# One 64 KB-per-partition load of wq, one loop for q, and matmuls on zeros ahead of q and of the scores

## The chip, the core and the metric

The kernel runs on one core of a Trainium2 chip. The metric is the device time of one execution in microseconds (us). Before the change three runs gave 98.8, 98.8 and 98.97 us; the median is 98.8 us. One further execution was recorded by the hardware profiler, and all rows below come from it.

## What is computed

One token (x has 1024 elements, all data bf16) goes through an attention branch and an MLP branch, and both are added to it:

```python
xn = layernorm(x)
q = xn @ wq                       # 1024 x 4096: 32 heads of 128
k, v = the last W = 4096 positions of the caches, 4 KV heads, each used by 8 query heads
p = softmax(q k^T * 128 ** -0.5)
attn = (p v) @ wo                 # 4096 x 1024
y = layernorm(xn)
mlp = gelu(y @ w1 + b1) @ w2 + b2 # 1024 x 3584 x 1024
out = x + attn + mlp
```

All of wq (8 MB), K and V (4 MB each), w1 and w2 (7 MB each) and wo (8 MB) must be read from the device memory: 39.86 MB in the profile. The arithmetic on one token is small beside that.

## The kernel before, in words

**Loads.** Nearly every load is issued by SP, in program order, into one queue. Each is one transfer over 128 partitions with one run of bytes per partition; `load_chunks` cuts a weight into chunks of rows. The order on SP is: the first half of wq (32 KB per partition), the first half of K (`load_k(0)`), the second half of wq, the second half of K, w1 (56 KB per partition), then V in two halves, w2 in two chunks, wo in four chunks (`WO_CHUNKS`), and the output. V is loaded into the buffer of K (`KV`), so SP waits for the last of the four transposes of K, `C["kt", 3]`, before V. w2 overwrites wq (both are in `BIG`), so SP waits for eight counts of `done["q"]`; wo overwrites w1, so SP waits for seven counts of `done["h"]`. Three small rows (x, b2 and b1) are issued by ACT on a queue of its own. Both queues are served by the same 16 DMA engines; each takes 8 of the 128 partitions of a large load.

**Engines.** POOL fills constants. ACT zeroes the PSUM banks 0, 1 and 7 by copying a zero tile. PE spreads x over 128 partitions with two matmuls (L426), DVE computes the layernorm statistics and puts the normalized x into `XZ` (L274): a zero tile of 136 columns for each of eight groups, in which a few columns hold x. PE multiplies windows of `XZ` with wq to get q in bank 7: 64 matmuls with a moving operand of 512 columns, in two passes over the halves of wq. A register named `turn` and a semaphore `s_feed`, which POOL raises as loads and transposes finish, let PE wait for the right stage inside a loop; the first two turns are the halves of wq.

DVE transposes K in four pieces (`turn_k`, L284), 4.4 us each, as the halves land: pieces 0 and 1 need the first half of K, 2 and 3 the second. Program order on DVE is piece 0, 1, 2, then the transpose of q (L292) and the copies into `QBD` (L303; ACT makes the other half, L305), then piece 3. The scores on PE are 32 matmuls in two groups of 16: the first needs `QBD` and pieces 0 and 1, the second piece 3. Ahead of them PE does four small matmuls for b1 (L446), two for x and b2 (L454) and four that write the mask of the two KV heads (L457, moving operand with 2 rows).

After the scores PE does w1 (56 matmuls, the loop that counts `done["h"]`), the sum of p, the turned h, p v (32 matmuls), seven rounds of eight matmuls on w2 and four rounds on the first chunk of wo, paced by `s_feed`, and at last the other chunks of wo: matmuls of 32 columns of weights (`OT`), one `s_wo` wait for each chunk; the last chunk, a single row of wo, uses weights that were loaded in advance (L517, L507). Then ACT and DVE copy the result out and SP stores it.

Of the kernel before, what the change touches and what calls it, by code (L numbers as in the profile page):

```python
# [18 lines left out]
KC = D // 128  # L19
NQ = HQ * DH  # L20
W1_CHUNKS = [8]
WQ_CHUNKS = [4, 4]
W2_CHUNKS = [16, 12]
WO_CHUNKS = [16, 11, 4, 1]
WO_HEAD = 1
XW = 136
PAIRS = 2
# [24 lines left out]
def bass_parallel_sum__sliding_block_cached__mixer_channel_mlp__decode_kernel(  # L52
# [17 lines left out]
    pe, dve, act, pool, sp = nc.tensor, nc.vector, nc.scalar, nc.gpsimd, nc.sync  # L70

    def sems(name, n):
        return [nc.alloc_semaphore(f"{name}{i}") for i in range(n)]

    s_x, s_b1, s_b2, s_v, s_out = (nc.alloc_semaphore(n) for n in ("s_x", "s_b1", "s_b2", "s_v", "s_out"))
    s_w1 = sems("s_w1", len(W1_CHUNKS))
    s_wq = sems("s_wq", len(WQ_CHUNKS))
    s_k = sems("s_k", PAIRS)
    s_wo = sems("s_wo", len(WO_CHUNKS))
    s_w2 = sems("s_w2", len(W2_CHUNKS))  # L80

    DVE = Track(nc, "S_DVE")
    ACT = Track(nc, "S_ACT")
    POOL = Track(nc, "S_POOL")
    done = {n: nc.alloc_semaphore(f"S_PE_{n}") for n in (
        "x", "h", "hT", "q", "sc", "pv", "tot", "fin")}
    s_feed = nc.alloc_semaphore("S_FEED")

    def sb(name, shape, d):
        return nc.alloc_sbuf_tensor(name, shape, d)  # L90
# [10 lines left out]
    OTHER = sb("OTHER", [2, 128], bf16)  # L101
    ALT = sb("ALT", [2, 512], bf16)
# [9 lines left out]
    XZ = sb("XZ", [128, KC * XW], bf16)  # L112
    YZ = sb("YZ", [128, 192], bf16)
    QBD = sb("QBD", [128, PAIRS * 512], bf16)
# [16 lines left out]
    GO = sb("GO", [128, ROUNDS * STEP + LEAD + 96], bf16)  # L131
# [6 lines left out]
    WA, W1 = BIG[:, 0:KC * NQ], BIG[:, KC * NQ:KC * NQ + KC * F]  # L138
    W2 = WA[:, 0:FC * D]
    PS = nc.alloc_psum_tensor("PS", [128, 8 * 512], f32)  # L140
    PSb = PS[:, :].bitcast(bf16)

    def bank(n, rows=128, first=0):
        return PS[first:first + rows, n * 512:(n + 1) * 512]

    w1_p = B_w1.rearrange("(p r) n -> p r n", r=KC)
    wq_p = A_wq.rearrange("(p r) n -> p r n", r=KC)
# [5 lines left out]
    C = {}  # L153

    def load_chunks(dst, src, chunks, width, semaphores, c0=0):
        for j, n in enumerate(chunks):
            sp.dma_start(  # L157
                dst[:, c0 * width:(c0 + n) * width].rearrange("p (c n) -> p c n", c=n),
                src[:, c0:c0 + n, :],
            ).then_inc(semaphores[j], 16)  # L160
            c0 += n
# [10 lines left out]
    def pool_wait():  # L172
        pool.wait_ge(POOL.sem, POOL.cnt)
# [53 lines left out]
    def pairs(cache, c):  # L227
        return cache[0, 2 * c:2 * c + 2, SK - W:SK, :].rearrange("g (m i) d -> m g (i d)", m=64)

    def load_k(c):  # L230
        sp.dma_start(KV[:, c * 8192:(c + 1) * 8192], pairs(A_k_cache, c)).then_inc(s_k[c], 16)  # L231

    load_chunks(WA, wq_p, WQ_CHUNKS[:1], NQ, s_wq)
    load_k(0)
    load_chunks(WA, wq_p, WQ_CHUNKS[1:], NQ, s_wq[1:], WQ_CHUNKS[0])
    load_k(1)
    load_chunks(W1, w1_p, W1_CHUNKS, F, s_w1)

# [59 lines left out]
    for b in range(4):  # L298
        for c in range(PAIRS):
            to = QD[32 * b:32 * b + 32, c, :, b, 16 * c:16 * c + 16].rearrange("p e (u j) -> p e u j", j=4)  # L300
# [5 lines left out]
    turn_k(3)  # L306

    V = KV[:, :]
    sp.wait_ge(DVE.sem, C["kt", 3])
    for c in range(PAIRS):  # L310
        sp.dma_start(V[:, c * 8192:(c + 1) * 8192], pairs(A_v_cache, c)).then_inc(s_v, 16)
    sp.wait_ge(done["q"], 8)
    load_chunks(W2, w2_p, W2_CHUNKS, D, s_w2)
    sp.wait_ge(done["h"], 7)
    c0 = 0
    for j, n in enumerate(WO_CHUNKS):
        first = (FC + c0) * D
# [79 lines left out]
    for engine, track, a in ((act, ACT, 1), (dve, DVE, 0)):  # L397
        engine.wait_ge(done["fin"], 1)
        of, to = PS[64 * a:64 * a + 64, 7 * 512 + 256 * a:7 * 512 + 256 * a + 256], Pb[0:64, 256 * a:256 * a + 256]
# [4 lines left out]


    pool_wait()
    pool.wait_ge(s_wq[0], 16)
    pool.sem_inc(s_feed, 1)
    pool.wait_ge(s_wq[1], 16)
    pool.sem_inc(s_feed, 1)  # L410
    pool.wait_ge(DVE.sem, C["kt", 1])
    pool.sem_inc(s_feed, 1)
    pool.wait_ge(DVE.sem, C["kt", 3])
    pool.sem_inc(s_feed, 1)
    for semaphores, chunks in ((s_w2, W2_CHUNKS), (s_wo, WO_CHUNKS[:WO_HEAD])):
        if semaphores is s_wo:
            pool.wait_ge(ACT.sem, C["OT"])
        for semaphore, n in zip(semaphores, chunks):
            pool.wait_ge(semaphore, 16)
            pool.sem_inc(s_feed, n // ROUND)  # L420
    pe.wait_ge(POOL.sem, C["ones"])
    turn = pe.alloc_register("turn")
    pe.reg_mov(turn, 1)
    pe.wait_ge(s_x, 16)
    for i in range(2):
        last = pe.matmul(bank(2 + i), lhsT=onesb[0:1, :], rhs=XB[0:1, 8 * i:8 * i + 8, :])  # L426
    last.then_inc(done["x"], 1)

    def add(to, lhsT, rhs, **place):
        return pe.matmul(to, lhsT=lhsT, rhs=rhs, start=False, stop=False, skip_group_check=True, **place)  # L430

    pe.wait_ge(DVE.sem, C["xz"])
    with pe.Fori(0, len(WQ_CHUNKS)) as j:
        pe.wait_ge(s_feed, turn)
        pe.reg_add(turn, turn, 1)
        with pe.Fori(0, 4) as t:
            for u in range(2):
                for k in range(4):
                    last = add(bank(7), XZ[:, bass.ds(t * 2 + j * (4 * XW) + (XW * k + u), 128)],
                               WA[:, bass.ds(t * -1024 + j * (4 * NQ) + (k * NQ + (7 - u) * 512), 512)])  # L440
            last.then_inc(done["q"], 1)

    pe.wait_ge(s_b1, 16)
    turned = PS[:, 2 * 512 + 32:2 * 512 + 64].rearrange("p (c t) -> p c t", c=4)[:, :, 0:7]
    for q in range(4):
        pe.matmul(turned, lhsT=E4[:, q * 128:(q + 1) * 128],  # L446
                  rhs=B1R[:, q * FC:(q + 1) * FC].rearrange("p (t c) -> p c t", c=4),
                  start=(q == 0), stop=False, skip_group_check=True)
# [4 lines left out]
    for a in range(2):  # L453
        pe.matmul(bank(7), lhsT=EDGE[:, 1 - a:129 - a], rhs=XB[:, 8 * a:8 * a + 8, :], start=(a == 0), stop=False,  # L454
                  skip_group_check=True)
    for n in range(4):
        pe.matmul(bank(3 + n), lhsT=OTHER[:, :], rhs=ALT[:, :], start=True, stop=False, skip_group_check=True)  # L457
    pe.wait_ge(DVE.sem, C["d_QBD"])
    K4 = KT[:, :].rearrange("p (x k) -> p x k", k=128)
    with pe.Fori(0, PAIRS) as c:  # L460
# [3 lines left out]
        with pe.Fori(0, 2) as j:  # L464
            for n in range(4):
                for u in range(2):
                    last = add(bank(3 + n), QBD[:, bass.ds(c * 512 + j * 256 + u * 128, 128)],
                               K4[:, bass.ds(c * 64 + 16 * n, 16), bass.ds(j * 64 + 32 * u, 32)])
                last.then_inc(done["sc"], 1)

    def h_cols(row, t):
        return row.rearrange("p (m a c) -> p m a c", m=128, a=7)[:, :, bass.ds(t, 1), :]

    pe.wait_ge(s_w1[0], 16)
    with pe.Fori(0, 7) as t:
        for k in range(KC):
            last = add(bank(0), YZ[:, bass.ds(t + 8 * k, 128)], h_cols(W1[:, k * F:(k + 1) * F], t))
# [5 lines left out]
    for c in range(4):  # L483
        last = add(turned[:, c], H8[:, c:512:4], FLIP[:, 0:7])
# [6 lines left out]
    with pe.Fori(0, 8) as i:  # L491
        for u in range(4):
            last = add(bank(1), PT[:, bass.ds(i * 256 + u * 64, 128)], V3[:, :, bass.ds(i * 1024 + u * 256, 256)])
# [12 lines left out]
    def add_held(to, lhsT, rhs, column):  # L506
        return pe.add_instruction(mybir.InstMatmult(  # L507
            name=nc.get_next_instruction_name(), engine=pe.engine, start_tensor_calc=False, stop_tensor_calc=False,
            tile_size=(128, 32), tile_position=(0, column), bass_skip_group_check=True, ldweights=False,
            ins=[pe.lower_ap(rhs), pe.lower_ap(lhsT, for_matmul_weights=True)], outs=[pe.lower_ap(to)]))  # L510

    for j, n in enumerate(WO_CHUNKS[WO_HEAD:]):
        held = c0 + n == 32
# [5 lines left out]
        for c in range(c0, c0 + n):  # L519
            rhs = BIG[:, (FC + c) * D:(FC + c + 1) * D]  # L520
            for a in range(4):
                first, column = LEAD + 2 * (c - TAIL) - (0 if a % 2 else ROW), 7 * 512 + a // 2 * 256
                to, of = PS[32 * a:32 * a + 32, column:column + 256], rhs[:, TAIL_AT[a]:TAIL_AT[a] + 256]
                if held:
                    last = add_held(to, OT[:, first:first + 32], of, 32 * a)
                else:
                    last = add(to, OT[:, first:first + 32], of, tile_position=(0, 32 * a))
# [32 lines left out]
```

## Time and profile before

| | us |
|---|---|
| Median of three runs | 98.8 |
| The profiled execution | 99.37 |
| Span of its rows on the core | 97.4 |
| PE busy | 73.0 |
| DVE busy | 38.9 |
| ACT busy | 11.2 |
| POOL busy | 9.9 |

The profiled execution took 1.97 us more than its span, which is start and end of the program outside the rows. HBM read is 39.86 MB, a mean of 409 GB/s over the span, and the large loads' packets took 95.7% of the time of the 16 DMA engines. In the list of idle times the entry behind an arrow is what ended the wait. PEclk is the granted share of the TensorE clock. A matmul with a moving operand of 512 columns follows the one before it after about 216 ns at the full clock and after 427 ns at half of it, as the starts of the rows show.

### The profile page before, as it was taken

What the parts mean: (1) busy time and instruction counts of PE and PEld (TensorE: products, weight loads), DVE (VectorE), ACT (ScalarE), POOL (GpSimd) and SP (SyncE); (2) the same over time, 40 slices, a digit from 0 to 9 for tenths busy, and PEclk for the clock granted to TensorE, in tenths of its full rate; (3) what the DMA queues carried; (4) which work ended last, traced back from release to release, by engine and by line L of the source; (5) the groups of instructions that cost most, each with busy time, mean ns of one, the idle gap of its engine ahead of it and who ended that gap; (6) DMA issues with size and microseconds to landing.
All of it is one profiled execution on the core that took longest, in us unless ns stands there. A gap on an engine that the chain in (4) does not pass through costs nothing.

```text
span 97.4 us, 1285 instructions
## 1 busy us (share of the span) xinstructions
PE 73.0 (75%) x354; PEld 30.4 (31%) x354; DVE 38.9 (40%) x54; ACT 11.2 (12%) x20; POOL 9.9 (10%) x27
## 2 busy tenths in 40 slices
PE   0004000099999986999979999799999999779992
PEld 0000000033444431333434444333343443334450
DVE  0002899899930799940293620050048000000001
ACT  0880000600000024000005200200000000000001
POOL 6999400000000000000000000000000000000000
PEclk9999999999999998557999999999999999999999
DMA  7599999999999998888999999999999999899890
GB/s 215 256 431 431 405 432 444 431 444 431 410 431 481 636 424 377 377 377 377 437 431 431 437 498 431 431 444 394 394 464 498 431 431 431 376 435 426 372 377 1
DMA packets 1989, 39.88 MB, mean 409 GB/s; under 512 B 322, under 2 KB 324, under 8 KB 452
## 3 DMA queue, kind: packets, MB, share of 16 engines
q1 hardware_dynamic: 1876, 39.85, 95.7%
q10 hardware_dynamic: 112, 0.01, 0.1%
q8 instruction: 1, 0.02, 0.1%
HBM read 39.86 MB, written 0.00 MB: 409 GB/s over the span
## 4 chain that ended last, share of the span: by engine, by line
DMA 80%; PE 14%; SPq 3%; issue 1%; DVE 0%
DMA BIG<-in_B_w_dram 47%; DMA BIG<-in_A_wo_dram 33%; PE PS L430 13%; SPq L231 1%; SPq L157 1%; SPq L318 1%; DVE Pb L400 0%; PE PS L507 0%
## 5 line engine op out<-in xcount | busy, mean ns | idle before, releaser
L430 PE MATMUL PS<-BIG,XZ 128*128 x64 | 16.5, 427 | 10.2 <-DVE B L277 10.2
L430 PE MATMUL PS<-BIG,GO 128*128 (+1 forms) x148 | 22.2, 337 | 1.4 <-POOLq L420 1.2
L284 DVE STREAM_TRANSPOSE KT<-KV 128x4096 bf16<-128x4096 bf16 x4 | 17.6, 4432 | 4.8 <-DMA KV<-in_A_k_cache_dram 4.8
L430 PEld LDWEIGHTS PS<-BIG,GO 128*128 (+1 forms) x148 | 9.9, 97 | 13.8 <-issue 6.4
L430 PEld LDWEIGHTS PS<-BIG,XZ 128*128 x64 | 6.9, 108 | 20.3 <-issue 14.3
L430 PE MATMUL PS<-BIG,YZ 128*128 x56 | 12.4, 380 | 0.6 <-DMA BIG<-in_B_w_dram 0.6
L430 PE MATMUL PS<-KT,QBD 128*128 x32 | 10.0, 491 | 1.0 <-ACT QBD L305 1.0
L430 PE MATMUL PS<-KV,KT 128*128 x32 | 8.3, 381 | 0.5
L400 DVE CAST Pb<-PS 64x256 bf16<-64x256 f32 x1 | 0.4, 417 | 20.4 <-PE PS L507 20.4
L430 PEld LDWEIGHTS PS<-BIG,YZ 128*128 x56 | 5.4, 96 | 7.6 <-issue 1.8
L426 PE MATMUL PS<-XBRP,onesb 1*128 1x512 bf16 x2 | 1.0, 616 | 8.1 <-DMA XBRP<-in_A_x_dram 8.1
L430 PEld LDWEIGHTS PS<-KT,QBD 128*128 x32 | 3.8, 120 | 7.2 <-issue 5.2
L244 DVE BATCH_NORM_STATS2 BN<-PS 128x6 f32<-128x512 f32 x2 | 1.3, 689 | 9.1 <-PE PS L426 9.1
L430 PEld LDWEIGHTS PS<-KV,KT 128*128 x32 | 3.1, 96 | 5.3 <-issue 3.8
L332 DVE TENSOR_REDUCE MX<-PS 128x1 f32<-128x1024 f32 x2 | 2.4, 1220 | 5.6 <-PE PS L430 5.6
L379 DVE SCALAR_TENSOR_TENSOR QBD<-PS,REC,HALF 32x256 f32<-32x256 f32 x2 | 0.9, 474 | 6.9 <-PE PS L430 6.8
L344 ACT ACTIVATE Pb<-PS,NMB 128x2048 bf16<-128x2048 f32 x1 | 2.0, 1968 | 13.8 <-DVE NMB L341 13.8
L348 DVE STREAM_TRANSPOSE KT<-Pb 128x2048 bf16<-128x2048 bf16 x1 | 2.3, 2311 | 2.1 <-ACT Pb L344 2.1
L353 DVE COPY HT<-PS 128x28 f32<-128x28 f32 x1 | 0.2, 210 | 6.4 <-PE PS L430 6.4
L400 ACT ACTIVATE Pb<-PS 64x256 bf16<-64x256 f32 x1 | 0.4, 381 | 20.1 <-PE PS L507 20.1
L426 PEld LDWEIGHTS PS<-XBRP,onesb 1*128 1x128 bf16 x2 | 0.1, 104 | 8.1 <-DMA XBRP<-in_A_x_dram 8.1
L290 ACT ACTIVATE Pb<-PS 128x512 bf16<-128x512 f32 x1 | 0.6, 597 | 16.6 <-PE PS L430 16.6
(77 smaller groups left out, 37.7 us busy)
## 6 DMA issues: line engine op xcount, KB each, us to landing
BIG<-in_A_wq_dram SPq DMA_DIRECT2D x2, 4096.0 KB, 18.8
BIG<-in_B_w_dram SPq DMA_DIRECT2D x1, 7168.0 KB, 46.0
KV<-in_A_k_cache_dram SPq DMA_DIRECT2D x2, 2048.0 KB, 23.1
KV<-in_A_v_cache_dram SPq DMA_DIRECT2D x2, 2048.0 KB, 13.6
BIG<-in_B_w_dram SPq DMA_DIRECT2D x1, 4096.0 KB, 24.8
BIG<-in_A_wo_dram SPq DMA_DIRECT2D x1, 4096.0 KB, 23.5
BIG<-in_B_w_dram SPq DMA_DIRECT2D x1, 3072.0 KB, 31.4
BIG<-in_A_wo_dram SPq DMA_DIRECT2D x1, 2816.0 KB, 29.8
```

The lines of the kernel that those rows point to most:

```text
L157: sp.dma_start(dst[:, c0 * width:(c0 + n) * width].rearrange("p (c n) -> p c n", c=n), src[:, c0:c0 + n, :],).then_inc(semaphores[j], 16)
L231: sp.dma_start(KV[:, c * 8192:(c + 1) * 8192], pairs(A_k_cache, c)).then_inc(s_k[c], 16)
L244: DVE.mark(dve.bn_stats(out=BN[:, 12 * n + 6 * i:12 * n + 6 * i + 6], in_=src[:, 512 * i:512 * i + 512]))
L284: C["kt", n] = DVE.mark(dve.transpose(KT[:, n * 4096:(n + 1) * 4096], KV[:, n * 4096:(n + 1) * 4096]))
L318: sp.dma_start(BIG[:, first:first + n * D], wo_flat[:, c0 * D:(c0 + n) * D]).then_inc(s_wo[j], 16)
L332: C["mx"] = DVE.mark(dve.tensor_reduce(out=MX2[:, n:n + 1], in_=S[:, 1024 * n:1024 * n + 1024], axis=AX.X, op=ALU.max))
L344: C["exp"] = ACT.mark(act.activation(out=Pb[:, :], in_=S, func=ACTF.Exp, bias=NMB[:, 0:1], scale=SCALE, accum_out=SUMP[:, 0:1]))
L348: C["d_pt"] = DVE.mark(dve.transpose(PT[:, 0:2048], Pb[:, :]))
L379: DVE.mark(dve.scalar_tensor_tensor(out=ONM.rearrange("p (i c d) -> p i c d", i=2, c=PAIRS)[:, i], in0=PS[rows, 512:1024].rearrange("p (c ...
L400: track.mark(act.activation(out=to, in_=of, func=ACTF.Copy) if a else dve.tensor_copy(to, of))
L426: last = pe.matmul(bank(2 + i), lhsT=onesb[0:1, :], rhs=XB[0:1, 8 * i:8 * i + 8, :])
L430: return pe.matmul(to, lhsT=lhsT, rhs=rhs, start=False, stop=False, skip_group_check=True, **place)
```

## The change

wq is loaded by one DMA (64 KB per partition) ahead of both halves of K. The loop for q has one level with eight rounds of eight matmuls, and waits for wq's and XZ's semaphores directly, no longer through POOL's feed. SP waits for transpose 1 of K before the first half of V and for transpose 3 before the second. wo's chunks are 16, 10, 5 and 1 rows in place of 16, 11, 4 and 1. Two groups of matmuls are added whose operands are zeros, with all 128 rows and 512 columns: 24 between the spreading of x and q (into bank 4, which the scores later overwrite), and two after each of the four mask matmuls (zeros are added to bank 1). The mask matmuls become a loop. PE waits for the zero tile QBD at its start and for POOL's constants after q.

```diff
-WQ_CHUNKS = [4, 4]
+WQ_CHUNKS = [8]
-WO_CHUNKS = [16, 11, 4, 1]
+WO_CHUNKS = [16, 10, 5, 1]
...
-    load_chunks(WA, wq_p, WQ_CHUNKS[:1], NQ, s_wq)
+    load_chunks(WA, wq_p, WQ_CHUNKS, NQ, s_wq)
     load_k(0)
-    load_chunks(WA, wq_p, WQ_CHUNKS[1:], NQ, s_wq[1:], WQ_CHUNKS[0])
     load_k(1)
     load_chunks(W1, w1_p, W1_CHUNKS, F, s_w1)
...
     V = KV[:, :]
-    sp.wait_ge(DVE.sem, C["kt", 3])
     for c in range(PAIRS):
+        sp.wait_ge(DVE.sem, C["kt", 2 * c + 1])
         sp.dma_start(V[:, c * 8192:(c + 1) * 8192], pairs(A_v_cache, c)).then_inc(s_v, 16)
...
-    pool.wait_ge(s_wq[0], 16)
-    pool.sem_inc(s_feed, 1)
-    pool.wait_ge(s_wq[1], 16)
-    pool.sem_inc(s_feed, 1)
     pool.wait_ge(DVE.sem, C["kt", 1])
...
-    pe.wait_ge(POOL.sem, C["ones"])
+    pe.wait_ge(POOL.sem, C["QBD"])
...
+    def busy(zeros, to, **how):
+        for i in range(2):
+            pe.matmul(to, lhsT=zeros[:, 0:128], rhs=zeros[:, 0:512], skip_group_check=True, **how)
+
+    with pe.Fori(0, 12):
+        busy(QBD, bank(4), start=True, stop=True)
+    for s in s_wq:
+        pe.wait_ge(s, 16)
     pe.wait_ge(DVE.sem, C["xz"])
-    with pe.Fori(0, len(WQ_CHUNKS)) as j:
-        pe.wait_ge(s_feed, turn)
-        pe.reg_add(turn, turn, 1)
-        with pe.Fori(0, 4) as t:
-            for u in range(2):
-                for k in range(4):
-                    last = add(bank(7), XZ[:, bass.ds(t * 2 + j * (4 * XW) + (XW * k + u), 128)],
-                               WA[:, bass.ds(t * -1024 + j * (4 * NQ) + (k * NQ + (7 - u) * 512), 512)])
-            last.then_inc(done["q"], 1)
-
+    with pe.Fori(0, 8) as t:
+        for k in range(KC):
+            last = add(bank(7), XZ[:, bass.ds(t + XW * k, 128)], WA[:, bass.ds(t * -512 + (k * NQ + 7 * 512), 512)])
+        last.then_inc(done["q"], 1)
+
+    pe.wait_ge(POOL.sem, C["consts"])
     pe.wait_ge(s_b1, 16)
...
-    for n in range(4):
-        pe.matmul(bank(3 + n), lhsT=OTHER[:, :], rhs=ALT[:, :], start=True, stop=False, skip_group_check=True)
+    with pe.Fori(0, 4) as n:
+        pe.matmul(PS[:, bass.ds(n * 512 + 3 * 512, 512)], lhsT=OTHER[:, :], rhs=ALT[:, :], start=True, stop=False,
+                  skip_group_check=True)
+        busy(GO, bank(1), start=False, stop=False)
```

## The prediction

> **What bounds the kernel now.** I read the page's busy slices and DMA queues first, then the chain that ended last, then the order of time on PE, DVE and SP around the change.
>
> The slices, forty of 2.4 us, and the queues:
>
> ```profile
> PE   0004000099999986999979999799999999779992
> PEclk9999999999999998557999999999999999999999
> DMA  7599999999999998888999999999999999899890
> q1 hardware_dynamic: 1876, 39.85, 95.7%
> ```
>
> The reader should see that the DMA row is full from slice 3 to slice 38 while PE has holes, and that the granted clock drops to half around slices 16 to 18. The trace's records of single packets make this exact. The first packet of SP's queue starts at 1.83 us, the last ends at 95.05 us, and in between all 16 engines are busy without a hole. A 16 KB packet takes 611 ns, a 32 KB packet 1213 ns, a 56 KB packet 2116 ns; from the last two, (2116 - 1213) ns for 24576 bytes is 27.2 bytes per ns, and 1213 - 32768 / 27.2 leaves about 9 ns for a packet whatever its size. 39.85 MB over 16 engines at 27.2 bytes per ns is 91.5 us of the 93.2 us; the rest is some 0.6 us in which each engine's first packet is late (1.8 us against 1.21), the small costs per packet, and 0.85 us between the first and the last engine to finish.
>
> The chain and the end of the order of time:
>
> ```profile
> 3.28 45.97 DMA BIG<-in_B_w_dram
> 62.92 31.79 DMA BIG<-in_A_wo_dram
> 93.23 1.10 PEld L430 LDWEIGHTS PS<-BIG,GO 128*32 128x32 bf16 x44 [0.42 <-issue]
> 94.76 0.34 PEld L430 LDWEIGHTS PS<-BIG,GO 128*32 128x32 bf16 x16 [0.43 <-DMA BIG<-in_A_wo_dram]
> 95.40 0.28 PE L507 MATMUL PS<-BIG,GO 128*32 128x256 bf16 x4
> 96.23 0.33 SPq L402 DMA_DIRECT2D out_dram<-Pb  x1
> ```
>
> The end is set by the last bytes of wo: the last packet ends at 95.05, its matmuls L507 start at 95.40, and copy and store follow. But PE is close behind. It waits 1.18 us at 85.92 for the first chunk of wo and 0.43 us at 94.76. If it came late at 85.92 and never waited, it would need from there 7.3 us (85.92 to 93.23) and 1.10 + 0.34 + 0.11 us for weight loads up to L507; counted from the end of the round before (84.74) that is 93.6 at the earliest, against 95.40. So PE may fall behind by about 1.7 us before the end moves, and every further microsecond counts whole.
>
> The stretch that the change rearranges:
>
> ```profile
> 8.08 1.03 PE L426 MATMUL PS<-XBRP,onesb 1*128 1x512 bf16 x2 [8.08 <-DMA XBRP<-in_A_x_dram]
> 18.22 0.24 DVE L274 CAST XZ<-XNT 128x32 bf16<-128x32 f32 x1
> 18.80 8.76 DVE L284 STREAM_TRANSPOSE KT<-KV 128x4096 bf16<-128x4096 bf16 x2
> 19.33 16.55 PE L430 MATMUL PS<-BIG,XZ 128*128 x64 [10.22 <-DVE B L277]
> 32.35 4.45 DVE L284 STREAM_TRANSPOSE KT<-KV 128x4096 bf16<-128x4096 bf16 x1 [4.79 <-DMA KV<-in_A_k_cache_dram]
> 36.72 0.67 DVE L292 STREAM_TRANSPOSE Pb<-Pb 128x512 bf16<-128x512 bf16 x1
> 38.14 4.45 DVE L284 STREAM_TRANSPOSE KT<-KV 128x4096 bf16<-128x4096 bf16 x1
> 38.99 10.04 PE L430 MATMUL PS<-KT,QBD 128*128 x32 [0.96 <-ACT QBD L305]
> 42.61 1.20 SPq L311 DMA_DIRECT2D KV<-in_A_v_cache_dram  x2
> 49.61 12.44 PE L430 MATMUL PS<-BIG,YZ 128*128 x56 [0.57 <-DMA BIG<-in_B_w_dram]
> ```
>
> q is 64 matmuls in 16.55 us, of which about 12 run at half clock (427 ns apart, up to 24.5 us). The scores are 32 matmuls in 10.04 us, 14 of them at half clock:
>
> ```profile
> 38.20:45.00 6.80, 6.01 (x15) 2.18 (x16) 4.39 (x1) 0.26 (x2) 0.00 (x0) 0.50 1.03 447
> ```
>
> This is the stretch at a granted clock of 0.50 (the column before DMA share and GB/s); PE was busy in 6.01 us of it and did 15 matmuls.
>
> **The change part by part.**
>
> *One load of wq.* Bytes are the same. Per engine 8 packets of 64 KB take the place of 16 of 32 KB, and one closing packet of 9 ns goes: 9 x 9 ns = 0.08 us off the stream at most; by starts, which overlap by 3 or 4 ns, 9 x 5 = 0.045 us. No 64 KB packet is in the trace. Its nearest row, 56 KB, is on the same straight line, so I take 0.07 us gained. Bounds: the 0.08 us, and on the other side that the lateness of an engine's first packet (0.6 us) grows with its size, which would cost 0.6 us. SP issues one DMA less (0.71 us of its time); it is ahead of the stream, w1 being issued at 3.28 and started after 31 us, so nothing comes of that.
>
> *x behind larger packets.* x, b2 and b1 share the engines. x's 128-byte packets start between 6.04 and 6.49 us, after three wq packets on each engine, and the closing ones after a fourth. With 64 KB packets the same places come at 1.83 + 3.05 + 2 x 2.41 = 9.7 us and 12.1 to 12.6 us, so PE gets x at about 12.9 us in place of 8.08; if x stands behind two packets only, at 10.5. The Trainium skill, "DMA: Bandwidth & Descriptors", section "Queues, rings and completion order", says that an engine alternates between queue rows packet by packet; the alternation agrees with these records, the three packets at first are more than it says. The chain on DVE from x to XZ takes 18.46 - 8.08 = 10.4 us, so XZ is ready at 23.3 us (20.9 in the milder case). I take 23.3.
>
> *q.* wq lands when both halves of K are still to come: K's second half landed at 32.3 at the same sum of bytes; 16 packets of 0.61 us earlier is 22.6. q is released by XZ, at about 24.1 with the 0.87 us that now lies between L274 and the first q matmul. All 64 at the full clock: 13.9 us, end at 38.0 (before: 35.88). With 12 at half clock, 40.6. The 24 zero matmuls start at 14.0, after x; at half clock all would take 10.2 us, until 24.2, and hide under the same wait; if the clock comes up they end around 21 to 22.
>
> *K later.* K's first half lands at 27.5 in place of before 18.8. DVE then transposes without waiting: 27.5 + 8.76 + 4.45 = 40.7. Only now comes L292, queued behind piece 2. It needs q's copy from bank 7, 0.6 us after q, 38.6 or 41.2: the first hides, the second costs 0.5 us. From L292 to the first score it took 38.99 - 36.72 = 2.27 us, so the scores start at 43.0 and not 38.99. Piece 3 runs 1.42 us behind L292, 42.1 to 46.6.
>
> *Zero matmuls before the scores.* PE does two rows for x and b2, then 4 mask and 8 zero matmuls after q's copy: 0.45 + 12 x 0.216 = 3.05 us, 38.6 to 41.7. They fit before 43.0. What they cost if q is late is one for one: the ready time of 43.0 is passed when q ends later than 39.3.
>
> *Scores.* At the full clock the first 16 take 3.5 us, until 46.5; the second 16 wait for piece 3 and POOL's feed, 46.8, and end at 50.3. w1 has landed at 49.25, so its loop starts at 50.35 where it started at 49.61: PE is 0.75 us late, inside the 1.7 us. At half clock the first 16 take 6.4 us as before, and the loop starts at 52.9: 3.3 us late, 1.6 us beyond the slack.
>
> Which it is hangs on the granted clock. Before, it fell at 38.20 although PE had no gap over 0.96 us since 35.88: what ran in between were matmuls of 2 or 32 rows or of 28 columns. It stayed up through 1.18 us of nothing at 84.74 and through 1 us of nearly nothing at 62.1. After the change the gaps are 0.7 us behind q and 1.3 us before the scores, with two thirds of the matmuls between them full-sized. I take it that the clock stays. The Trainium skill, "TensorE: Matmul & The Clock Gate", section "Why this matters for your kernels", asks for no gaps above some 3 us. By that rule alone the clock would have held before, which the row at 0.50 contradicts; by the rule the sum here would be the one without a late PE, by the row it is open.
>
> *V, w2, wo.* SP issues the first half of V at piece 1 (36.3), the second and w2 at piece 3 (46.6, done by 48.8). The stream is in w1 until about 49, then has 4.9 us of V's first half: no hole. wo waits for the w1 loop, 62.9 or 65.4 in place of 62.06; w2 keeps the stream until about 75: no hole. Without that cover, each microsecond late would be one in the end.
>
> *Chunks of wo.* 10 and 5 rows land with the same bytes before the last row. After the fifth row's landing PE has 20 in place of 16 matmuls, 4 x 0.021 = 0.08 us; the weight loads then end at 95.29, before L507's 95.40: nothing. *Waits on PE at start*: QBD's zeros are filled at 2.03, hidden under the wait for x.
>
> Sum: -0.07 us. The profiled execution would be 99.37 - 0.07 = 99.3, and the median, 0.57 below it before, 98.8 - 0.07 = 98.73, say 98.7.
>
> **Rivals.**
>
> *PE becomes the bound (slower).* The place is the granted clock at the first scores, or before it at q. For it: the 0.50 row, and that operands of zero may not count as work, of which the trace has no row of its own kind; XZ is nearly all zeros, but wq moving through is not. Against: the zero matmuls have full shape, and a third of a window of thin ones was what went wrong before. The price is 1.6 us with 14 cold matmuls, 0.3 with 8; it decides from the point where w1's loop starts later than 51.3. Time: 98.8 + 1.6 - 0.07 = 100.3, or from 99.0.
>
> *The engines' ends draw together (faster).* The last engine ends 0.85 us after the first. If fewer and larger packets halve this, 0.4 us go: 98.3. For it: first packets ended between 3.6 and 4.07, a spread that could be recast. Against: the bytes and starts per engine are the same.
>
> *The merged load is split again or starts slower.* Split into two packets each it gives 98.8, a first packet late in proportion 98.8 + 0.6 - 0.07 = 99.3. Against the latter: engines that started late (2.43) had a first packet only 0.2 us late, so the lateness goes by the clock, not by bytes. The Trainium skill, "DMA: Bandwidth & Descriptors", section "Anatomy of one DMA", gives about 2.0 us fixed per DMA. By that, one DMA fewer would give 96.8; the stream without holes says that this is hidden, and I leave it 1 in 100.
>
> **Chances.** The forecast 0.49 (with the split, 98.6 to 98.9), PE late 0.34, ends drawn together or the fixed cost 0.14, slow start 0.03. 0.2% is 0.2 us, about what a measurement of this kernel can tell from no change. Faster 0.15, same 0.48, slower 0.37. The forecast's own range is 98.6 to 98.9; for 8 in 10 the range goes to the faster rival's 98.4 and to the slower one's 100.3.
>
> **What would show it.** Right: 128 packets of 64 KB at about 2417 ns; x's matmuls at about 12.9; L292 at 40.7; scores from 43.0 in about 7.3 us with the granted clock at 1.00; w1's loop before 51.3; waits of PE for wo still there at about 86 and 94.7. Wrong: a granted clock of 0.50 in the scores or in q beyond the zero matmuls, no wait for wo at 86, L507 later than 95.5; or a last packet clearly before 94.9.

## The result: slower by 0.8%, and the profile after

The changed kernel takes 99.64 us (median of six runs, 99.27 to 100.01) beside 98.82 us for the kernel before in the same session; the ratio is 1.0083, with a 95% interval of 1.0064 to 1.0102. The forecast was 98.7 us and no change that can be measured. The rival in which PE becomes the bound is what happened, though not for the reason that it gave.

The busy slices and the clock of the changed kernel, forty slices of 2.45 us:

```profile
PE   0000599914999999899799999979999999999992
PEclk9999999999579999999999999999999999999999
DMA  9399999979999998889799999998999999999960
```

The trace has records of the granted clock only from 17.82 us on (in the kernel before from 24.55 on), and the row shows 9 where it has none. Up to there the matmuls start 427 ns apart, which is the pace of half the clock, so for the first stretch the pace is what to read.

And the end of its order of time (start, length, engine, instruction):

```profile
94.52 1.54 PEld L425 LDWEIGHTS PS<-BIG,GO 128*32 128x32 bf16 x60 [0.42 <-issue]
96.06 0.10 PEld L518 LDWEIGHTS <-GO 128*32 128x32 bf16 x4
96.17 0.28 PE L508 MATMUL PS<-BIG,GO 128*32 128x256 bf16 x4
97.00 0.33 SPq L401 DMA_DIRECT2D out_dram<-Pb  x1
```

The 9s of PE now run unbroken from slice 27 on. The 60 small matmuls on wo stand in one piece, where before there was a wait of 0.43 us for a chunk of wo among them, and the wait of 1.18 us at 86 is gone too. L508 starts at 96.17; its counterpart L507 started at 95.40. That is 0.77 us, and the span grew by 0.8.

The chain that ended last by shares of its lines; in the kernel before it had been w1's load up to 49.25 us, w1's loop on PE, and wo's load from 62.92 to 94.71:

```profile
PE PS L425 67%; DMA BIG<-in_A_wq_dram 23%; PE PS L429 2%; PE PS L456 1%; ACT Pb L289 1%; PE PS L453 1%; ACT H L349 1%; DVE Pb L399 0%; PE PS L508 0%
```

Pieces of that chain in order of time (start, length, what):

```profile
0.81 22.25 DMA BIG<-in_A_wq_dram
...
23.41 15.67 PE PS L425 x64
...
47.23 0.63 issue
...
52.12 12.45 PE PS L425 x56
```

The chain is now wq's load and then PE to the end. Read it with care: it goes back to the instruction before on the same engine where a wait is short, so it runs through q, though the experiments below show that q could have been 1.6 us faster for nothing. The order of time around K shows where PE became late:

```profile
10.85 1.03 PE L421 MATMUL PS<-XBRP,onesb 1*128 1x512 bf16 x2 [10.85 <-DMA XBRP<-in_A_x_dram]
11.81 8.30 PE L429 MATMUL PS<-QBD 128*128 128x512 bf16 x24
23.41 15.66 PE L425 MATMUL PS<-BIG,XZ 128*128 x64 [3.30 <-DMA BIG<-in_A_wq_dram]
27.80 13.10 DVE L283 STREAM_TRANSPOSE KT<-KV 128x4096 bf16<-128x4096 bf16 x3 [6.12 <-DMA KV<-in_A_k_cache_dram]
40.82 0.67 DVE L291 STREAM_TRANSPOSE Pb<-Pb 128x512 bf16<-128x512 bf16 x1
42.24 4.45 DVE L283 STREAM_TRANSPOSE KT<-KV 128x4096 bf16<-128x4096 bf16 x1
43.52 3.71 PE L425 MATMUL PS<-KT,QBD 128*128 x16
47.87 4.07 PE L425 MATMUL PS<-KT,QBD 128*128 x16 [0.63 <-issue]
52.12 12.44 PE L425 MATMUL PS<-BIG,YZ 128*128 x56 [0.18 <-issue]
```

DVE has no K before 27.80 and then never stops: three pieces, the transpose of q, the copies, the fourth piece, which ends at 46.69 (before: 42.59). The second group of scores starts 1.18 us after that, takes 4.07 us, and w1's loop starts at 52.12 in place of 49.61. From there everything on PE is 2.5 us late.

The 1.18 us look like a wait for the fourth piece over POOL's feed, and they are not. These two lines are POOL's instruction that raises the feed for the fourth piece, and the instruction on PE's sequencer (PEldq here, with the register and branch instructions between the matmuls) that waits for the feed, once for each group, with the first and the last start:

```profile
L409 POOLq EVENT_SEMAPHORE  x1: 17/17/17, 46.7 to 46.7; - x1
L463 PEldq ALU_OP  x2: 36/36/36, 42.4 to 47.3; - x2
```

By the trace's records of instructions and semaphores POOL raises the feed at 46.74, 0.05 us after the piece. The sequencer comes to it at 47.29, and starts there 0.06 us after its instruction before, as it did for the first group, whose feed had stood for long. So it waited neither for the piece nor for POOL: the first group's last matmul starts only at 46.85, and the turn of the loop follows. The last thing that the sequencer did wait for is ACT's half of `QBD`, at 42.60. Between there and w1's loop stand only the scores and the turns of their loops.

The scores run at the full clock, as the zero matmuls were to ensure; q does not. The granted clock is the number before the DMA share in these stretches:

```profile
20.10:23.40 3.30, 0.01 (x1) 0.02 (x1) 1.24 (x6) 1.69 (x3) 0.00 (x0) 1.00 0.51 219
24.60:28.10 3.50, 3.50 (x10) 1.18 (x8) 0.30 (x1) 0.00 (x0) 0.00 (x0) 0.51 1.01 431
43.50:52.10 8.60, 7.70 (x33) 2.99 (x32) 4.17 (x2) 0.00 (x0) 0.00 (x0) 1.00 0.91 394
```

The zero matmuls ahead of q end at 20.1, PE waits 3.3 us for wq, and the clock is halved from 24.65 to 28.06.

### The profile page after: what moved, and what is told of

Read it like the earlier page. It is cut to its first block, busy times and chain, and to the rows that moved or that the text cites. A ratio compares the mean times of both kernels' runs of the same rounds, so it can differ in the third digit from the quotient of the medians.

```text
span 98.2 us, 1365 instructions
## 1 busy us (share of the span) xinstructions
PE 79.2 (81%) x375; PEld 33.0 (34%) x386; DVE 38.9 (40%) x54; ACT 11.2 (11%) x20; POOL 9.9 (10%) x27
## 4 chain that ended last, share of the span: by engine, by line
PE 71%; DMA 23%; issue 3%; ACT 1%; DVE 0%
PE PS L425 67%; DMA BIG<-in_A_wq_dram 23%; PE PS L429 2%; PE PS L456 1%; ACT Pb L289 1%; PE PS L453 1%; ACT H L349 1%; DVE Pb L399 0%; PE PS L508 0%
## 5 line engine op out<-in xcount | busy, mean ns | idle before, releaser
L425 PE MATMUL PS<-BIG,GO 128*128 (+1 forms) x137 | 21.3, 333 | 0.7
L425 PE MATMUL PS<-BIG,XZ 128*128 x64 | 15.7, 410 | 3.3 <-DMA BIG<-in_A_wq_dram 3.3
L429 PE MATMUL PS<-QBD 128*128 128x512 bf16 x24 | 8.3, 528 | 0.0
L425 PE MATMUL PS<-KT,QBD 128*128 x32 | 7.7, 379 | 0.7 <-issue 0.6
L429 PEld LDWEIGHTS PS<-QBD 128*128 128x128 bf16 x24 | 3.0, 129 | 5.6 <-issue 4.7
L425 PEld LDWEIGHTS PS<-KT,QBD 128*128 x32 | 3.1, 96 | 5.2 <-issue 2.6
## 6 DMA issues: line engine op xcount, KB each, us to landing
BIG<-in_B_w_dram SPq DMA_DIRECT2D x1, 7168.0 KB, 46.8
```

The costliest lines, as they stand in the source:

```text
L429: pe.matmul(to, lhsT=zeros[:, 0:128], rhs=zeros[:, 0:512], skip_group_check=True, **how)
```

## The experiments

The question is what made PE late: K behind wq, the clock in q, the packets of 64 KB, or the zero matmuls themselves. Every ratio is to the kernel before in the same session, with its 95% interval.

**36 zero matmuls ahead of q.** They reach to 21.4 us.

```diff
-    with pe.Fori(0, 12):
+    with pe.Fori(0, 18):
         busy(QBD, bank(4), start=True, stop=True)
```

> The changed kernel with 36 zero matmuls ahead of q in place of 24, so that they reach to wq's landing. Theory A (PE is late because K is late: DVE's transposes start at 27.8 and the transpose of q stands behind the third of them): q runs at the full clock and ends about 1.6 us earlier, at 37.4, but the first score still starts at about 43.1 and w1's loop at about 51.7 in place of 52.12; the time falls by some 0.4 us only, to 99.2. Theory B (the clock that falls in q is the cause): PE gains the whole 1.6 us and the time is that of the kernel before, 98.8, or what the stream of loads gives, 99.1.

99.47 us (99.37 to 99.61), ratio 1.0049 (1.0030 to 1.0068). From this run's order of time:

```profile
23.46 13.97 PE L425 MATMUL PS<-BIG,XZ 128*128 x64 [2.08 <-DMA BIG<-in_A_wq_dram]
40.89 0.67 DVE L291 STREAM_TRANSPOSE Pb<-Pb 128x512 bf16<-128x512 bf16 x1
43.17 4.13 PE L425 MATMUL PS<-KT,QBD 128*128 x16 [1.12 <-ACT QBD L304]
47.93 4.12 PE L425 MATMUL PS<-KT,QBD 128*128 x16 [0.63 <-issue]
52.20 12.44 PE L425 MATMUL PS<-BIG,YZ 128*128 x56 [0.15 <-issue]
```

The clock did not fall: the trace has no record of a change, and all 64 matmuls of q start 216 ns apart. The gap of 2.08 us before q was not enough to lower it, and q ended 1.6 us earlier. The transpose of q still starts at 40.89, behind the third piece of K, and w1's loop at 52.20. So the clock in q is not the cause: theory B falls. Whether it accounts for a part of the scatter is not shown: in the runs of the changed kernel with a mean clock of 0.983 the times are 99.27 to 99.58, in those with 0.965, which is one more slow stretch at a place that is not known, 99.7 to 100.01. With 36 zero matmuls they lie between 99.37 and 99.61, the two runs with a mean of 0.965 (99.40 and 99.52) among them.

**wq in two loads, both still ahead of K.**

```diff
-WQ_CHUNKS = [8]
+WQ_CHUNKS = [4, 4]
```

> The changed kernel with wq in two loads of 32 KB per partition, both still ahead of K; q waits for both. Theory A (order of the loads): wq complete at about 22.8, K's first half at about 27.6, w1's loop starts at 52 to 53, time 99.6 to 100.2. Theory C (packets of 64 KB are the cause, by x's delay and by the late start of the stream): x is back at 8.1, the last packet of wo back at 95.05, and the time back at 98.8.

99.67 us (99.26 to 100.14), ratio 1.0066 (1.0044 to 1.0088). From the order of time of the profiled run, 100.14 us:

```profile
23.25 16.92 PE L425 MATMUL PS<-BIG,XZ 128*128 x64 [7.23 <-DMA BIG<-in_A_wq_dram]
27.68 13.10 DVE L283 STREAM_TRANSPOSE KT<-KV 128x4096 bf16<-128x4096 bf16 x3 [8.57 <-DMA KV<-in_A_k_cache_dram]
52.69 12.44 PE L425 MATMUL PS<-BIG,YZ 128*128 x56 [0.18 <-issue]
```

x is back at 8.27 us, but K's first transpose starts at 27.68, and w1's loop at 52.69. The order of the loads suffices for the loss, packets of 64 KB are not needed: theory C falls as the main cause. This execution is the slowest of its eleven, and one thing more made it late: x came early, so the zero matmuls ended 7.23 us before q, the clock was halved for 10 us, q ended at 40.1, and the mask loop behind it, not `QBD`, held the first scores until 44.62. So q's slack is short: an end at 39.0 cost nothing, an end at 40.1 some 0.5 us of w1's start.

**The kernel before with both groups of zero matmuls** (and the waits for POOL that they need).

```diff
...
+    with pe.Fori(0, 12):
+        busy(QBD, bank(4), start=True, stop=True)
     pe.wait_ge(DVE.sem, C["xz"])
...
-    for n in range(4):
-        pe.matmul(bank(3 + n), lhsT=OTHER[:, :], rhs=ALT[:, :], start=True, stop=False, skip_group_check=True)
+    with pe.Fori(0, 4) as n:
+        pe.matmul(PS[:, bass.ds(n * 512 + 3 * 512, 512)], lhsT=OTHER[:, :], rhs=ALT[:, :], start=True, stop=False,
+                  skip_group_check=True)
+        busy(GO, bank(1), start=False, stop=False)
```

> The kernel before with both groups of zero matmuls and nothing else. Theory A: the loads keep their order, so K is not late; q or the scores get faster, PE waits longer for w1 at 49.6 and for wo at 86, and the stream sets the end: 98.8, within 0.1. Theory D (the zero matmuls and their loop cost time by themselves): slower by 0.3 us or more.

98.93 us beside 98.91, ratio 0.9996 (0.9980 to 1.0012). They cost nothing where K is early, and win nothing, since the stream of loads is the bound. From this run's order of time:

```profile
44.24 4.07 PE L430 MATMUL PS<-KT,QBD 128*128 x16 [0.21 <-issue]
49.79 12.43 PE L430 MATMUL PS<-BIG,YZ 128*128 x56 [1.48 <-DMA BIG<-in_B_w_dram]
86.04 9.46 PE L430 MATMUL PS<-BIG,GO 128*128 x92 [1.14 <-POOLq L420]
```

The scores end early and the gain turns into a longer wait for w1 (1.48 us, before 0.57).

**The changed kernel without the zero matmuls before the scores.**

```diff
         pe.matmul(PS[:, bass.ds(n * 512 + 3 * 512, 512)], lhsT=OTHER[:, :], rhs=ALT[:, :], start=True, stop=False,
                   skip_group_check=True)
-        busy(GO, bank(1), start=False, stop=False)
```

> The changed kernel without the eight zero matmuls after the masks. If the zero matmuls hold the clock: granted clock 0.50 in the scores, their first 16 take 6.4 us and not 3.7, w1's loop starts at about 54.4, time about 101.3. If they only cost time: scores start at 43.1 in place of 43.5 at the full clock, time 99.2 to 99.3.

100.2 us (99.41 to 100.83), ratio 1.0108 (1.0064 to 1.0153). The order of time of the profiled run, 100.83 us:

```profile
43.57 9.96 PE L425 MATMUL PS<-KT,QBD 128*128 x32 [0.48 <-issue]
...
53.36 12.44 PE L425 MATMUL PS<-BIG,YZ 128*128 x56
```

and its stretch from 43.5 us, with the granted clock before the DMA share:

```profile
43.50:50.00 6.50, 6.43 (x17) 2.37 (x18) 3.13 (x1) 0.00 (x0) 0.00 (x0) 0.54 0.89 386
```

The clock is halved through most of the scores, and w1's loop starts at 53.36. So these eight matmuls on zeros can hold the clock, and in the two profiled runs that is worth 1.2 us of PE's time, where PE is the bound. The mean clock of the six runs goes from 0.931 (100.14 to 100.83 us) to 0.965 (99.41 and 99.50), so the fall does not hit every execution equally. The intervals of this kernel and the changed one overlap.

**The changed kernel without the zero matmuls ahead of q.**

```diff
-    with pe.Fori(0, 12):
-        busy(QBD, bank(4), start=True, stop=True)
```

> The changed kernel without the 24 zero matmuls ahead of q. If they are worth anything in the changed kernel, q then starts at half clock for one to two windows in every run, ends at 39.5 to 41, and the scores with their zero matmuls start up to 1.5 us later: 99.7 to 100.5, above the changed kernel beside it. If they came too early to matter (they end at 20.1, q starts at 23.4): the changed kernel's 99.3 to 100.0 again.

99.5 us (99.25 to 99.97), ratio 1.0059 (1.0039 to 1.0079), not told from the changed kernel with them. They came too early to matter, and q has slack until DVE is free for its transpose.

**K's first two pieces transposed only in half**, on top of the 36 zero matmuls; the half that is left out is filled with zeros, so a part of the scores is not computed. Once with wq in one load, once in two (with 52 zero matmuls).

```diff
-        C["kt", n] = DVE.mark(dve.transpose(KT[:, n * 4096:(n + 1) * 4096], KV[:, n * 4096:(n + 1) * 4096]))
+        width = 2048 if n < 2 else 4096
+        C["kt", n] = DVE.mark(dve.transpose(KT[:, n * 4096:n * 4096 + width], KV[:, n * 4096:n * 4096 + width]))
...
+    for n in range(2):
+        POOL.mark(pool.memset(KT[:, n * 4096 + 2048:(n + 1) * 4096], 0.0))
     pool_wait()
     pool.wait_ge(DVE.sem, C["kt", 1])
```

> The changed kernel with 36 zero matmuls ahead of q (e3), and pieces 0 and 1 of K transposed only in half (the other half of each is filled with zeros by POOL, so half of the first two heads' scores are left out). DVE gains 4.4 us of 17.8. Theory A (the queue of DVE behind the late K is the cause): piece 2 waits for K's second half (32.6), q's transpose follows at about 38.2, the scores start at 40.5, piece 3 ends at 44.1, w1's loop starts at about 50 and PE waits for wo again at 86; the time is the stream's, 98.9 to 99.2. If DVE's queue is not the cause: 99.5 as in e3.

> The same with wq in two loads of 32 KB per partition ahead of K, and 52 zero matmuls since x comes earlier. PE is early, so the time is the stream's. If packets of 64 KB make the stream late by some 0.2 us, this is 98.8 to 98.9 and 0.2 below the run with short transposes and one load; if its lateness is chance from start to start, the two are equal.

With one load 99.09 us, ratio 1.0003 (0.9985 to 1.0020); with two 98.92 us, ratio 0.9992 (0.9973 to 1.0010), beside 98.95 for the kernel before. The loss is gone in both. The order of time with one load:

```profile
39.48 4.45 DVE L284 STREAM_TRANSPOSE KT<-KV 128x4096 bf16<-128x4096 bf16 x1
45.59 4.12 PE L428 MATMUL PS<-KT,QBD 128*128 x16 [0.18 <-issue]
49.86 12.43 PE L428 MATMUL PS<-BIG,YZ 128*128 x56 [0.15 <-issue]
86.18 8.60 PE L428 MATMUL PS<-BIG,GO 128*128 x72 [1.23 <-POOLq L418]
```

All loads are as in the changed kernel; only DVE has less to do after K's late landing. The last piece ends at 43.9 and not 46.75, w1's loop starts at 49.86, and PE waits for wo again, 1.23 us as before. This shows theory A. The 0.17 us between the two medians goes the way that a later stream with 64 KB packets would go, but the intervals overlap. The last packet of the stream points the same way: it ended at 95.26 to 95.40 us in the five profiled runs with 64 KB, and with 32 KB first at 95.05 to 95.18 in six and at 95.33 in the run with two loads in front, leaving out one that is told below, in which an engine was delayed. It is not settled.

**PE made late in the kernel before.** Zero matmuls between the scores and w1 (8 and 16, written out), then in a loop behind w1 (6 and 12).

```diff
+    for i in range(16):
+        add(bank(1), GO[:, 0:128], GO[:, 0:512])
     pe.wait_ge(s_w1[0], 16)
...
+    with pe.Fori(0, 6):
+        for i in range(2):
+            add(bank(1), GO[:, 0:128], GO[:, 0:512])
     pe.wait_ge(ACT.sem, C["exp"])
```

> The kernel before with 8 full-sized zero matmuls (1.73 us at the full clock) between the scores and w1's loop. By the slack worked out in the prediction (1.7 us) w1's loop starts at about 50.8 in place of 49.61, PE's wait for wo at 86 shrinks from 1.18 to about 0, and the time stays at 98.8, within 0.1. If PE had no slack: 98.8 + 1.2 = 100.0.

> The kernel before with 16 such matmuls (3.46 us). w1's loop starts at about 52.5, 2.9 us late; 1.7 us are absorbed, so the time is about 98.8 + 1.2 = 100.0, with no wait for wo left. If the late PE of the changed kernel is not its cause, 98.8.

> The kernel before with a loop of 6 zero matmuls between w1 and the sum of p: PE is 1.3 to 1.4 us later from there on, whatever the clock did before, and wo is issued as early as before. With a slack of 1.7 us: no change, 98.9 beside a kernel before of 98.9, PE's wait at 86 almost gone.

> The same with 12 zero matmuls, 2.6 to 2.7 us. With a slack of 1.7 us: 0.9 to 1.0 us slower, L507 at about 96.4 and no wait for wo left. If the time goes by the stream alone: no change.

Eight written-out matmuls gave 98.78 to 101.23 us (ratio 1.0041, 1.0009 to 1.0074), 16 gave 100.22 (ratio 1.0135, 1.0107 to 1.0164), 6 in a loop 98.89 (0.9991, 0.9975 to 1.0008) and 12 in a loop 98.92 (1.0003, 0.9982 to 1.0024). None of them measures the slack. In the profiled run with 8 the scores ended early and the matmuls fit into the wait for w1. With 16, w1's loop started at 51.18, inside the slack, and yet the end came 1.3 us later; the wait for wo was still there. Its order of time:

```profile
51.18 12.44 PE L430 MATMUL PS<-BIG,YZ 128*128 x56
87.30 9.46 PE L430 MATMUL PS<-BIG,GO 128*128 x92 [0.33 <-POOLq L420]
96.73 0.27 PE L509 MATMUL PS<-BIG,GO 128*32 128x256 bf16 x4
```

The packet records point to the reason: a packet of 16 KB on the instruction queue, which in the kernel before comes at 94.85 us, with the end of the stream, came at 79.10 here, and one of the 16 DMA engines was some 1.2 us late from then on (its part of wo's first chunk ended at 86.56, the others' by 85.35; its last packet ended at 96.33, the others' by 95.07). The packet came earlier in the run with 16 matmuls written out, and in no other profiled run. Whether that is also what scatters the run with 8 is open. In the loop behind w1, 12 matmuls took 2.75 us, but the rounds on w2 started at 72.73 and not 71.88, 0.85 us later: the wait for ACT's copy of h ran beside them, and the loop for p v, whose sequencer leaves gaps, took 7.61 in place of 8.74 us. My expectation of 0.9 us there was wrong. This run shows one thing more. Its clock did not fall in the scores, which are those of the kernel before:

```profile
38.95 4.11 PE L430 MATMUL PS<-KT,QBD 128*128 x16 [1.08 <-ACT QBD L305]
43.69 4.12 PE L430 MATMUL PS<-KT,QBD 128*128 x16 [0.62 <-issue]
```

At the full clock they take 8.86 us from the first start to the end, where 32 x 0.216 us are 6.9. In the profiled run of the kernel before, 14 of them at half clock, they took 10.04.

The slack can be read from the other runs. Start of w1's loop, and of the last matmuls (L507 or its counterpart), us:

| Kernel | w1's loop | last matmuls | waits for wo left |
|---|---|---|---|
| before | 49.61 | 95.40 | yes |
| short transposes, two loads | 49.88 | 95.49 | yes |
| short transposes, one load | 49.86 | 95.67 | yes |
| no zeros ahead of q | 52.10 | 96.10 | no |
| changed | 52.12 | 96.17 | no |
| 36 zeros | 52.20 | 96.20 | no |
| two loads in front | 52.69 | 96.73 | no |
| no zeros before the scores | 53.36 | 97.41 | no |

From 52.1 on the end follows w1's loop one for one, 44.0 us behind it; that line meets 95.40 at 51.4, which is 1.8 us of slack.

**Smaller first loads in the kernel before.** K's first half ahead of wq; and wq in chunks of 2, 2, 4 and of 1, 3, 4 rows, two of them ahead of K (POOL's first feed then waits for both).

```diff
+    load_k(0)
     load_chunks(WA, wq_p, WQ_CHUNKS[:1], NQ, s_wq)
-    load_k(0)
...
-WQ_CHUNKS = [4, 4]
+WQ_CHUNKS = [2, 2, 4]
...
-    load_chunks(WA, wq_p, WQ_CHUNKS[:1], NQ, s_wq)
+    load_chunks(WA, wq_p, WQ_CHUNKS[:2], NQ, s_wq)
     load_k(0)
-    load_chunks(WA, wq_p, WQ_CHUNKS[1:], NQ, s_wq[1:], WQ_CHUNKS[0])
+    load_chunks(WA, wq_p, WQ_CHUNKS[2:], NQ, s_wq[2:], 4)
```

> The kernel before with K's first half (16 KB per partition) ahead of wq's first half. If the stream's late start grows with the size of its first packets (first packets 0.6 us late with 32 KB, up to 1.1 us with 64 KB), it shrinks with 16 KB: x lands at about 6, the last packet of wo ends 0.1 to 0.3 us before 95.05, and the time is 98.5 to 98.7. If the late start does not depend on the size: 98.8.

> The kernel before with wq in chunks of 2, 2 and 4 rows, the first two (16 KB per partition each) in front of K's first half. If the stream's late start goes with the size of the first packets (64 KB costs about 0.17 us against 32 KB), 16 KB may win 0.05 to 0.15 us: 98.75 to 98.85 beside a kernel before of 98.9. If only 64 KB is special, or the packets' own cost eats it: equal.

> The same with chunks of 1, 3 and 4 rows, the first packets 8 KB. As above, at most 0.2 us gained; slower only if the first packets end before the next load's descriptors are there, which would show as a hole in the stream at about 2.5 to 4 us.

K first: 99.51 us, ratio 1.0057 (1.0036 to 1.0078). Its first packet starts at 2.47 us in place of 1.83, and the last ends at 95.77 in place of 95.05: the late start of 0.64 us comes out at the end, as it must where the stream is the bound. The idea that 16 KB packets bring x at about 6 us failed here: x's packets went ahead of the late stream, and x was there at 2.72. Chunks of 2, 2, 4: 98.93 us, ratio 1.0013 (0.9993 to 1.0034); of 1, 3, 4: 98.86 us, ratio 1.0004 (0.9984 to 1.0024), beside 98.89. Nothing measurable is gained by smaller first packets, and no version was found that beats the kernel before.

## Why the prediction was wrong, point by point

**The bound.** The stream bounds the kernel before, and the end is PE's once PE is late enough: right, with a slack of 1.7 us predicted (its own figures, 95.40 less 93.6, give 1.8) and 1.8 read from the table.

**One load of wq.** -0.07 us predicted. The 64 KB packets took 2418 ns, as the straight line gave (2417), but the last packet of the stream ended at 95.33 and not 95.05. The first packets took up to 3.5 us; the last engine began at 3.07 against 2.43, which is scatter in part (2.49 to 3.21 in the profiled runs with 64 KB first, 2.27 to 2.78 with 32 KB). Once PE was early again the cost was between nothing and 0.2 us. The gain was not to be seen. Neither did a saving by one DMA fewer show, nor the rival in which the engines' ends draw together: the last packet came later and not earlier.

**x.** 12.9 us predicted, 10.85 measured: the milder case, with two wq packets ahead of x. The Trainium skill, "DMA: Bandwidth & Descriptors", section "Queues, rings and completion order", lets an engine alternate between queues packet by packet; after the first packets it did, and x landed at 5.75, 6.95, 8.08 and 10.85 us with first packets of wq of 8, 16, 32 and 64 KB.

**q.** Released by wq (its load landed at 23.06, predicted 22.6) and not by XZ; started at 23.41 and ended at 39.0, between the two predicted cases. That the clock would stay was wrong for q. The Trainium skill, "TensorE: Matmul & The Clock Gate", section "Why this matters for your kernels", asks for no gap above some 3 us: here 3.3 us lowered the clock, and so did 2.98 us in the kernel before with both groups of zeros, while 2.08 us with 36 zero matmuls did not. By that rule the fall in q was within reach in advance, from the gap of 2 to 3 us that the prediction's own times left. But it cost next to nothing, as the prediction's own bound said: q may end as late as 39.3.

**K later.** Right: 27.5 predicted and 27.80 measured for the first transpose, 40.7 and 40.82 for the transpose of q.

**Scores: the step that failed.** The prediction gave 16 scores 16 x 0.216 = 3.5 us, and had "the second 16 wait for piece 3 and POOL's feed, 46.8, and end at 50.3", some 7.3 us from 43.0 for all 32. Piece 3 ended at 46.69 and the feed was up at 46.74, as predicted, but the second 16 began at 47.87 and w1's loop at 52.12. What was too small is the price of 32 scores at the full clock, which left out PE's sequencer and the turns of its two loops. Where the first score had waited for `QBD`, they took 8.88 us with 36 zero matmuls and 8.86 in the kernel before with 12 zero matmuls behind w1. In the second group of the changed kernel, matmuls start 216 ns apart within a turn of eight, the first of a turn 314 ns before the next, and 480 ns lie between the turns, so 16 take 4.07 us; from the last start of the first group to the first of the second it is 1.01 us. In the profile before this was not to be seen: 14 of the 32 ran at half clock, 427 ns apart, and the other 18 followed 216 ns apart, all without a gap. The sequencer seems to have run ahead in the slow stretch.

Against the prediction the second group is 1.07 us late, and its length with the loop's own start makes another 0.70, together 1.8 us. This turns the 0.75 us of lateness into 2.5, and 2.5 less the slack is the 0.8 us measured. The order, the late K and the slack were right, and this one size decided the sign.

**Zero matmuls before the scores.** Predicted to end at 41.7; their loop takes 0.86 us a turn and ended at 43.7, so the first scores came at 43.52, and at 43.17 where q was early. It does not matter, since the sequencer ran on meanwhile: the second group began 7.05 us after the start of q's transpose in one run and 7.04 in the other.

**The slower rival.** Its place, PE behind the wait for wo, was right, and its point of decision (51.3) too. Its cause, a cold clock in the scores, was wrong in the changed kernel and right in the one without the zero matmuls.

**V, w2, wo and the chunks.** No hole in the stream from any of them, as predicted; the chunks of 10 and 5 rows changed nothing that can be seen.

## What to carry to other kernels

Where two bounds are 1.7 us apart, every moved step needs its price with everything between two instructions in it: the sequencer and the loops' turns made 8.9 us of scores that were counted as 7.3. A time that stands between two events is not yet a wait: the hop over POOL's semaphore, which the 1.18 us suggest, took 0.05. Loading one operand in larger pieces pushes back the next, and the one to look at is the engine that has to prepare it, here 18 us of transposes on DVE that could no longer start while the other load ran. A matmul time taken from a stretch at half clock hid the sequencer's share here, so it could not be halved for the full clock.

## What the runs showed of the hardware that was not expected

Matmuls on zeros, both operands zero, can raise and hold the clock: the 24 ahead of q begin 427 ns apart, and go on at 216 ns from 18.0 us; with the eight before the scores the clock is 1.00, without them 0.54 over the first 6.5 us. It is not certain in each execution: in the profiled run with short transposes and two loads the clock fell from 40.04 to 43.45 in spite of the eight, and in the one with 12 zero matmuls behind w1, which has none before the scores, it stayed up. The masks' matmuls with a moving operand of 2 rows did not hold it in the kernel before, nor in the changed kernel without the eight.

A packet of 16 KB on the instruction queue can delay the loads. At 94.85 us it was harmless; in the run where it came at 79.10 us, one engine was 1.2 us late from then on, and L509 came 1.3 us after L507 of the kernel before. That run has 16 written-out matmuls more.

What is loaded first can shift the start of the stream: with K's first half in front, its first packet came at 2.47 us, 0.64 us later than wq's did. It is not the size, since wq's 16 KB in front began at 1.84; whether it is K's access pattern, with two heads side by side, was not tested.
